# Token groups of 512, 512, 512, 384, 384 in place of 384, 512, 512, 512, 384, with the work order laid anew

## The chip, the cores and the metric

The kernel runs on one core of one Trainium2 chip. The metric is the device time of one execution in microseconds; the kernel before took 482.29 us (median of 3 runs, 481.82 to 482.75). The profile is of one more execution, which took 482.01 us; its span, from the first to the last instruction that the profile holds, is 480.2 us.

## The reference

Three layers follow one another, over 4 batches of 576 tokens (2304 in all) with 8 heads of 64, so 512 channels. `factor` is 4 and `scale` 1/8.

```
# 1. attention, twice: over tokens averaged by 4 (then repeated 4 times), and over neighbours |i-j| < 4
out_d = sm_attn(mean4(q), mean4(k), mean4(v));  out_up = repeat(out_d, 4)
scores = where(|i-j| < 4, scale * q @ k.T, -1e9);  attn = exp(scores - max) / (sum + 1e-9)
x = out_up + attn @ v                                   # (2304, 512)
# 2. gated layer: d_ff = 1536
x = ((x @ w_a) * (x @ w_b)) @ w_out                     # (2304, 512)
# 3. soft mixture of 8 experts with 4 slots each, F = 1024
logits = x @ phi                                        # (2304, 32)
d = softmax(logits, over tokens);  slot_in = d.T @ x    # (32, 512)
slot_out[e] = relu(slot_in[e] @ w1[e]) @ w2[e]
out = softmax(logits, over slots) @ slot_out            # (2304, 512)
```

w_a, w_b and w_out come as 64-bit numbers and are turned into 32-bit ones on the chip.

## The kernel before

**Attention** goes by pairs: each batch has five stretches of up to 116 tokens (`plan_pair`). A pair is scored on PE (L462, L472), reduced and exponentiated on DVE and ACT (L480 to L506), normalized on POOL or DVE (L293), transposed on PE (L516), multiplied with v on PE (L530), and added to the coarse attention of its batch (`xadd`, L541, DVE). Then x is split into a high part (a rounded copy, `xhi`) and the rest (a subtraction, `xlo`), on ACT, DVE or POOL. The coarse attention of a batch (`plan_datt`) must be done before its first pair is multiplied with v: its scores are L673, its exponentials L701 (ACT), its transposes L733 and L737, its product L784.

**The gated layer** goes by groups of tokens, `GS`, and 12 slices of 128 of d_ff. One unit (`plan_unit`) is a group and a slice: 12 matmuls for w_a and 12 for w_b (L1068), each 128 by the group's tokens, then a copy on ACT or DVE and a multiplication on DVE (L1083) into one of the chunks of the tile `gr`. A unit can begin when the whole group's x is there, so the first one waits for all pairs of the first group. The order in which a group takes its 12 slices is turned by `KO`, and `GO` says at which chunk of `gr` it begins.

**The weights** w_a and w_b come in 24 pieces of 512 KB (`plan_piece`): a DMA into a staging slot, two steps on ACT or DVE (`clow`, L877 or L879; `mag`, L883), one that joins them on DVE (L888), a rounded copy (`chi`, L288 or L290), and a subtraction (`clo`, L293, on POOL or DVE). Four pieces serve two units.

**The end**: after the last unit come the softmax over tokens, the slots' input (L1396), the experts (L1437, L1490) and the output (L1529). The experts' weights, 64 loads of 512 KB (L1343), go into buffers that the gated layer has left.

**The order** is written out: each step is a task with a number, `ORDER` lists all numbers, and each engine runs its tasks in that order; `OTHER` lists the tasks that run on their second engine. SP's queue of DMAs is in that order too. While PE has nothing to do in the first 60 us of the planner's count, the planner puts in matmuls on data that nobody reads (L347), as many as fill its own estimate of the gap; after the last unit it puts in others (L352).

Of the kernel before, what the change touches and what calls it, by code (L numbers as in the profile page):

```python
# [22 lines left out]
GS = [384, 512, 512, 512, 384]  # L23
# [4 lines left out]
GO = [0, 1, 0, 1, 0]  # L28
KO = [0, 6, 0, 9, 0]
NGC = 5  # L30
# [9 lines left out]
HEADS = [0, 2, 4, 6, 1, 3, 5, 7]  # L40
# [77 lines left out]
def rows_of(w):  # L118
    w = w.view(np.int64) if w.dtype == np.float64 else w
    return np.ascontiguousarray(w.reshape(8, 64, -1)[HEADS].reshape(w.shape))  # L120
# [128 lines left out]
def tile_attn_glu_softmoe(  # L249
# [16 lines left out]
    nc = tc.nc  # L266
    ctx.enter_context(tc.manual_schedule())
    P = Plan(dict(CAPS))
    add = P.add
# [38 lines left out]
    def c_dma(nbytes, wide=False):  # L308
        return nbytes / (400e3 if wide else 358e3)
# [15 lines left out]
    gr = mp.tile([128, NGC * 1536], F32, name="gr")  # L325
# [10 lines left out]
    T = {}  # L336
# [259 lines left out]
    def room_of(where):  # L596
        if where == "w8":
            return sb(wp, "w8", (128, 1024))
        if where == "sw":
            return X["sw"].pop(0).bitcast(F32)  # L600
        n = int(where[2:])
        return gr[:, n * 1536:n * 1536 + 1024]
# [264 lines left out]
    wsrc = (w_a, w_b)  # L867
# [25 lines left out]
    def plan_piece(n, key):  # L893

        fc, m = key[0], key[-1]
# [4 lines left out]
        def stage():  # L900
            X["raw", key] = s = X[where].pop(0)
            if isw:
                c0 = fc * 512 + key[2] * 256
                nc.sync.dma_start(
                    out=s.rearrange("p (m f) -> p m f", m=2),
                    in_=wsrc[key[1]][m * 256:m * 256 + 256, c0:c0 + 256].rearrange("(m p) f -> p m f", p=128),
                )
            else:
                nc.sync.dma_start(out=s, in_=w_outt[m * 128:m * 128 + 128, fc * 512:(fc + 1) * 512])
# [34 lines left out]
        o = CPR[n]  # L944
# [5 lines left out]
        if n == 0:  # L950
            T["stage"] = add("N", 0.0, rooms, (), -100, acq=("w8",) * CAPS["st"], lat=0.0)
        ts_ = add(
            "D", c_dma(524288), stage, [T["stage"]], prio=SOON[n] if n < len(SOON) else o - 1.5, acq=(where,), lat=2.0
# [99 lines left out]
    def plan_unit(g, k, n):  # L1053
        fc, fi = divmod(k, 4)
        gt = GS[g]
# [57 lines left out]
        tg = add("V", gt / 960 + 0.08, gmul, [tb, te, T.get(("gt", g, before))], -30, acq=tuple(f"gc{x}" for x in new), rel=("ps", "a", "un"))  # L1113
# [486 lines left out]
DE_AT = ["w8", "gc3", "sw", "sw"]  # L1600
PT_AT = ["w8", "gc4", "sw", "sw"]
# [11 lines left out]
def cpr(c):  # L1613
# [122 lines left out]
```

## Time and profile before

| | |
|---|---|
| median of 3 runs | 482.29 us |
| the profiled execution | 482.01 us |
| its span | 480.2 us |
| PE busy | 466.8 us, 97% |
| DVE, ACT, POOL busy | 269.4, 145.4, 121.6 us |
| first matmul of the gated layer, and the second | 38.05 us, 39.38 us |
| last matmul of the gated layer's last unit | issued at 420.4 us |
| moved by DMA | 84.26 MB |

The page gives the busy time of each engine, the chain of work that ended last, and groups of instructions by line. The tables by stretch of time give busy time, the clock granted to TensorE and the DMA engines' busy share. A matmul's end is modelled, so a time from the start of one instruction to the start of the next is more exact than a duration.

### The profile page before, as it was taken

Reading aid. Unit: us, or ns where it says so; the run is one execution under the profiler, and the core shown is the slowest. Engines: PE = TensorE matmul, PEld = TensorE weight load, DVE = VectorE, ACT = ScalarE, POOL = GpSimd, SP = SyncE. Lnnn points to the kernel's source line nnn. Section 1 sums busy time; section 2 is a strip of 40 time slices with the busy share of each in tenths; the row PEclk is TensorE's granted clock in tenths of the full one; section 3 lists DMA queues with packets and bytes.
Section 4 is the critical chain, followed back from the end, with each engine's and each line's share of the span. In section 5 each row is a group of like instructions: output and inputs, shape, how many; then the busy total and the mean of one; then the engine's idle time right before and its main releaser. Section 6 shows DMA issues by size and latency. Waiting matters only on the chain.

```text
span 480.2 us, 11383 instructions
## 1 busy us (share of the span) xinstructions
PE 466.8 (97%) x4755; PEld 363.0 (76%) x4755; DVE 269.4 (56%) x570; ACT 145.4 (30%) x392; POOL 121.6 (25%) x180
## 2 busy tenths in 40 slices
PE   7999999999999999999999999999999999999994
PEld 4778989887776777778788777788877879853462
DVE  3998997485658545678543249423525743460022
ACT  1878846514244311221320113002120210321132
POOL 4888985443055000454050011000000000010000
PEclk9999999999999999999999999999999999999998
DMA  8979843474651003223010010021236699899998
GB/s 303 389 264 306 291 132 115 139 240 176 217 173 45 2 1 114 58 65 128 12 46 0 18 50 1 3 87 45 97 129 240 216 363 377 283 346 410 407 407 322
DMA packets 30402, 84.26 MB, mean 175 GB/s; under 512 B 3472, under 2 KB 4240, under 8 KB 30352
## 3 DMA queue, kind: packets, MB, share of 16 engines
q1 hardware_dynamic: 30352, 83.54, 49.4%
q8 instruction: 37, 0.61, 0.5%
q14 instruction: 13, 0.11, 0.1%
HBM read 78.81 MB, written 4.72 MB: 174 GB/s over the span
## 4 chain that ended last, share of the span: by engine, by line
PE 84%; DVE 7%; ACT 4%; DMA 3%; issue 1%; SPq 0%; POOL 0%; ACTq 0%; DVEq 0%; POOLq 0%
PE ps L1068 58%; PE ps L1490 3%; PE ps L1437 3%; PE ps L1228 3%; PE ps L1093 3%; PE ps L530 2%; DMA w<-in_moe_w_dram 2%; PE ps L516 2%; DMA x<-in_qk_dram 1%; PE ps L784 1%; PE ps L673 1%; PE ps L472 1%; DVE dT L425 1%; PE ps L1529 1%; ACT ps L883 1%
## 5 line engine op out<-in xcount | busy, mean ns | idle before, releaser
L1068 PE MATMUL ps<-x,w 128*128 128x512 f32 (+1 forms) x1440 | 308.5, 371 | 1.2 <-DVE x L293 0.9
L1068 PEld LDWEIGHTS ps<-x,w 128*128 128x128 f32 x1440 | 259.8, 188 | 43.6 <-issue 5.5
L1083 DVE TENSOR_TENSOR gr<-a,ps 128x512 f32<-128x512 f32 (+1 forms) x60 | 37.7, 629 | 77.3 <-PE ps L1068 69.3
L288 ACT COPY a<-ps 128x512 f32<-128x512 f32 (+1 forms) x38 | 20.0, 534 | 95.8 <-PE ps L1068 93.9
L1101 DVE STREAM_TRANSPOSE gr<-gr 128x1024 f32<-128x1024 f32 (+2 forms) x31 | 33.1, 1089 | 5.3 <-PE ps L1093 5.3
L1215 POOL TENSOR_TENSOR cn<-lc,cs 128x128 f32<-128x128 f32 (+1 forms) x5 | 1.9, 380 | 133.1 <-DVE cs L1212 133.1
L293 POOL TENSOR_TENSOR x<-xn,x 128x464 fp32r<-128x464 f32 (+4 forms) x12 | 13.1, 1091 | 84.4 <-DVE x L290 73.6
L499 ACT ACTIVATE e<-e 128x512 f32<-128x512 f32 x20 | 12.6, 631 | 47.0 <-DVE e L492 47.0
L541 DVE TENSOR_TENSOR xn<-ps,xd 128x232 f32<-128x232 f32 (+1 forms) x40 | 13.8, 387 | 20.3 <-PE ps L530 19.9
L290 DVE COPY a<-ps 128x512 f32<-128x512 f32 (+1 forms) x22 | 14.1, 643 | 19.4 <-PE ps L1068 19.4
L293 POOL TENSOR_TENSOR w<-w,w 128x512 fp32r<-128x512 f32 x16 | 21.0, 1327 | 2.8 <-ACT w L288 2.5
L293 POOL TENSOR_TENSOR e<-e,mx 128x512 f32<-128x512 f32 x12 | 12.9, 1073 | 25.4 <-DVE mx L506 23.9
L347 PE MATMUL ps<-acc 128*128 128x512 f32 (+2 forms) x46 | 16.7, 494 | 2.2 <-POOL acc L340 2.2
L480 DVE TENSOR_REDUCE mx<-ps 128x4 f32<-128x256 f32 x40 | 14.7, 410 | 3.8 <-PE ps L472 3.8
L1228 PE MATMUL ps<-gr,lgs 32*32 32x384 f32 x576 | 16.3, 491 | 0.1
L530 PEld LDWEIGHTS ps<-e,bv 64*64 64x64 f32 x640 | 12.6, 133 | 4.9 <-issue 3.3
L425 DVE TENSOR_REDUCE dT<-qk 128x116 f32<-128x464 f32 (+1 forms) x20 | 12.0, 620 | 6.1 <-DMA qk<-in_qk_dram 6.1
L430 POOL TENSOR_TENSOR dT<-dT,qk 128x116 f32<-128x116 f32 (+1 forms) x28 | 14.7, 524 | 2.2
L530 PE MATMUL ps<-e,bv 64*64 64x58 f32 (+1 forms) x640 | 14.9, 226 | 0.1
L347 PEld LDWEIGHTS ps<-acc 128*128 128x128 f32 x46 | 8.7, 207 | 8.1 <-issue 5.2
L883 ACT ACTIVATE ps<-sw 128x512 f32<-128x512 f32 x18 | 11.4, 633 | 11.0 <-DVE xn L541 4.8
L492 DVE TENSOR_TENSOR e<-ps,mx 128x256 f32<-128x256 f32 x40 | 14.7, 409 | 0.0
(204 smaller groups left out, 568.9 us busy)
## 6 DMA issues: line engine op xcount, KB each, us to landing
w<-in_moe_w_dram SPq DMA_DIRECT2D x32, 512.0 KB, 8.7
qk<-in_qk_dram SPq DMA_DIRECT2D x17, 480.0 KB, 4.7
sw<-in_w_outt_dram SPq DMA_DIRECT2D x12, 512.0 KB, 3.8
w8x<-in_moe_w_out_dram SPq DMA_DIRECT2D x12, 512.0 KB, 3.7
x<-in_moe_w_dram SPq DMA_DIRECT2D x11, 512.0 KB, 7.9
w<-in_moe_w_a_dram SPq DMA_DIRECT2D x10, 512.0 KB, 7.3
bv<-in_vw_dram SPq DMA_DIRECT2D x20, 256.0 KB, 3.3
w8x<-in_moe_w_dram SPq DMA_DIRECT2D x10, 512.0 KB, 9.9
```

The lines of the kernel that those rows point to most:

```text
L288: nc.scalar.copy(out=out, in_=in_)
L293: (nc.vector if e == "V" else nc.gpsimd).tensor_tensor(**a)
L347: nc.tensor.matmul(out=X["warm"][:, 0:128 * w], lhsT=x[:, 0:128], rhs=x[:, 0:128 * w], start=True, stop=True)
L425: nc.vector.tensor_reduce(out=dst, in_=view(src, dims, off), op=ALU.add, axis=AX.X)
L430: nc.gpsimd.tensor_tensor(out=dst, in0=dst, in1=one[r], op=ALU.add)
L480: nc.vector.tensor_reduce(out=mx[:, hl], in_=X["s", n, hl], op=ALU.max, axis=AX.X)
L530: nc.tensor.matmul(out=pss[hl][o:o + 64, hq // 2, bi * w:bi * w + w], lhsT=v[r, bi, hq, :], rhs=pt[r, hq, 1 + bi * 64:1 + bi * 64 + w], st ...
L883: nc.scalar.activation(out=f, in_=words(raw)[0].bitcast(F32), func=ACTF.Prelu, scale=2.0 ** -112, alpha=-(2.0 ** 32))
L1068: nc.tensor.matmul(out=ps, lhsT=X["w", fc, ab, fi // 2, wi][:, fi % 2, hq, :], rhs=X[x, g][:, hq, :], start=(hq == 0 and m == 0), stop=(hq ...
L1083: nc.vector.tensor_tensor(out=X["g", g][:, k, :], in0=X.pop(("a", g, k)), in1=X.pop(("mm", g, k, 1)), op=ALU.mult)
L1101: nc.vector.transpose(out=t, in_=t)
L1228: nc.tensor.matmul(out=ps[q][o:o + 32, :], lhsT=d[r, b, :], rhs=g[r, :, b * 32:b * 32 + 32], start=(b < 4), stop=(b >= gt // 32 - 4),)
```

## The change

The first group has 512 tokens in place of 384 and the fourth 384 in place of 512. `GO`, `KO` and the order of the tasks are set anew, and some tasks go to other engines. A piece of w_a or w_b is now laid out on the host so that it is one run of 4 KB for each of the 128 partitions; before it was two runs of 2 KB. Since the first group now takes four chunks of `gr`, only the fifth is left beside it for buffers of the first pairs' batches: two of these are both put into the fifth chunk, at its start (up to 704) and behind (704 to 1280), with a new token `gp4` that the second group's unit takes when it begins to use that chunk.

```diff
-GS = [384, 512, 512, 512, 384]
+GS = [512, 512, 512, 384, 384]
-GO = [0, 1, 0, 1, 0]
-KO = [0, 6, 0, 9, 0]
+GO = [0, 1, 0, 2, 0]
+KO = [0, 9, 0, 8, 0]
 def rows_of(w):
     w = w.view(np.int64) if w.dtype == np.float64 else w
-    return np.ascontiguousarray(w.reshape(8, 64, -1)[HEADS].reshape(w.shape))
+    w = w.reshape(8, 64, -1)[HEADS].reshape(2, 2, 128, 3, 2, 256)
+    return np.ascontiguousarray(w.transpose(3, 4, 0, 2, 1, 5)).reshape(-1, 512)
 def room_of(where):
-        n = int(where[2:])
-        return gr[:, n * 1536:n * 1536 + 1024]
+        n = int(where[2:]) * 1536
+        return gr[:, n + 704:n + 1280] if where[1] == "p" else gr[:, n:n + 704]
 def stage():
-                c0 = fc * 512 + key[2] * 256
-                nc.sync.dma_start(
-                    out=s.rearrange("p (m f) -> p m f", m=2),
-                    in_=wsrc[key[1]][m * 256:m * 256 + 256, c0:c0 + 256].rearrange("(m p) f -> p m f", p=128),
-                )
+                r0 = (fc * 4 + key[2] * 2 + m) * 128
+                nc.sync.dma_start(out=s, in_=wsrc[key[1]][r0:r0 + 128, :])
 def plan_unit(g, k, n):
-  acq=tuple(f"gc{x}" for x in new)
+  acq=tuple(f"gc{x}" for x in new) + (("gp4",) if g == 1 and int(PT_AT[1][2:]) in new else ())
-DE_AT = ["w8", "gc3", "sw", "sw"]
-PT_AT = ["w8", "gc4", "sw", "sw"]
+DE_AT = ["w8", "gc4", "sw", "sw"]
+PT_AT = ["w8", "gp4", "sw", "sw"]
 ORDER = [
-    5, 8, 7, 11, 0, 1, 2, 10, 6, 12, 9, 14, 15, 3, 59, 61, 17, 13, 529, 16, 18, 530, 74, 76, 20, 62, 19, 27, 29, 37,
+    11, 5, 8, 7, 6, 12, 1, 0, 9, 529, 15, 10, 13, 18, 14, 3, 2, 59, 530, 27, 17, 61, 20, 16, 532, 531, 19, 21, 29, 62,
...
-CAPS.update({f"gc{x}": 1 for x in range(NGC)})
+CAPS.update({f"gc{x}": 1 for x in range(NGC)}, gp4=1)
```

The orders below leave times out. In the changed kernel the line numbers up to 904 are one higher, and those of the gated layer two lower (L1068 is L1066, L1529 is L1527).

PE before, the last rows ahead of the first unit (the band's four short matmuls that stand before each score of 16 are left out): v products (`e,bv`), scores (`qk`), transposes (`cst,e`) and matmuls on unread data (`acc`).

```order
L347 MATMUL ps<-acc 128x512
L347 MATMUL ps<-acc 128x256
L347 MATMUL ps<-acc 128x128
L530 MATMUL ps<-e,bv 64x58 x16
L516 MATMUL ps<-cst,e 128x128 x4
...
L472 MATMUL ps<-qk 58x64 x16
L530 MATMUL ps<-e,bv 64x58 x16
...
L472 MATMUL ps<-qk 58x64 x16
L347 MATMUL ps<-acc 128x256
L347 MATMUL ps<-acc 128x128
L1068 MATMUL ps<-x,w_277 128x384 x2
```

The same place in the changed kernel.

```order
L348 MATMUL ps<-acc 128x256
L348 MATMUL ps<-acc 128x128
L517 MATMUL ps<-cst,e 128x128 x4
...
L473 MATMUL ps<-qk 58x64 x16
L348 MATMUL ps<-acc 128x128
L531 MATMUL ps<-e,bv 64x56 x16
L348 MATMUL ps<-acc 128x256
L348 MATMUL ps<-acc 128x128
...
L473 MATMUL ps<-qk 58x64 x16
L1066 MATMUL ps<-x,w_345 128x512 x2
```

Ahead of the first unit there now stand a fifth v product (the one of 56 columns), a fifth transpose of a pair and an eighth score (before: four, four and seven). Counted in 128 columns, the `acc` matmuls ahead of it are 63 (before 57), of them 22 behind the first v product (before 13).

DVE before, around the first unit: the last x subtraction of the first group is `x<-xn,x 128x4x36`; `w` rows belong to the weights' pieces.

```order
L888 SCALAR_TENSOR_TENSOR w_143<-ps,w_143 128x512
L541 TENSOR_TENSOR xn<-ps,xd 128x232 x2
L888 SCALAR_TENSOR_TENSOR w_148<-ps,w_148 128x512
L290 CAST x<-xn 128x4x36
L293 TENSOR_TENSOR x<-xn,x 128x4x36
L425 TENSOR_REDUCE dT_684<-qk 128x4x29
L480 TENSOR_REDUCE mx<-ps 128x4 x2
L888 SCALAR_TENSOR_TENSOR w_144<-ps,w_144 128x512
L888 SCALAR_TENSOR_TENSOR w_145<-ps,w_145 128x512
```

DVE in the changed kernel, from the last x subtraction of the first group on.

```order
L294 TENSOR_TENSOR w_618<-w_103,w_617 128x2x256
L542 TENSOR_TENSOR xn<-ps,xd 128x2x112 x2
L291 CAST x<-xn 128x4x48
L294 TENSOR_TENSOR x<-xn,x 128x4x48
L426 TENSOR_REDUCE dT_435<-qk 128x4x29
L889 SCALAR_TENSOR_TENSOR w_105<-ps,w_105 128x512
L294 TENSOR_TENSOR w_746<-w_102,w_745 128x2x256
L889 SCALAR_TENSOR_TENSOR w_101<-ps,w_101 128x512
L291 COPY a<-ps 128x512
L889 SCALAR_TENSOR_TENSOR w_100<-ps,w_100 128x512
L294 TENSOR_TENSOR w_810<-w_105,w_809 128x2x256
L294 TENSOR_TENSOR w_746<-w_101,w_745 128x2x256
```

Up to the last x subtraction DVE has joined five weight pieces (before seven). In the whole program 11 of the weights' subtractions (`w` from `w` or `sw`) run on DVE (before 3); POOL has 13 (before 21).

PE at the end of the program, the changed kernel first: expert matmuls (`acc`), output matmuls (`cn,ht`), and the sum over experts of the last 128 columns (`a,cst`).

```order
L1527 MATMUL ps<-cn,ht 128x288 x4
L1488 MATMUL ps<-w_4645,acc 32x128 x8
L1488 MATMUL ps<-w_4078,acc 32x128 x8
L1488 MATMUL ps<-w_4079,acc 32x128 x8
L1488 MATMUL ps<-w_4230,acc 32x128 x8
L1527 MATMUL ps<-cn,ht 128x288 x4
L1508 MATMUL ps<-a,cst 128x128
L1527 MATMUL ps<-cn,ht 128x288 x8
```

Before, the rows from the second expert piece on were these.

```order
L1529 MATMUL ps<-cn,ht 128x288 x4
L1490 MATMUL ps<-w_4267,acc 32x128 x8
L1490 MATMUL ps<-x,acc 32x128 x8
L1490 MATMUL ps<-w_4599,acc 32x128 x8
L1490 MATMUL ps<-w_4526,acc 32x128 x8
L1510 MATMUL ps<-a,cst 128x128
L1529 MATMUL ps<-cn,ht 128x288 x8
```

Four output matmuls moved from before the expert matmuls to behind them, ahead of the sum over experts.

## Rows read from the trace of the kernel before

**Rows 1.** The page, part 1: busy us, share of the span, instructions.

```profile
PE 466.8 (97%) x4755; PEld 363.0 (76%) x4755; DVE 269.4 (56%) x570; ACT 145.4 (30%) x392; POOL 121.6 (25%) x180
```

**Rows 2.** Stretches: length; PE, PEld, DVE, ACT, POOL busy; clock; DMA share; GB/s.

```profile
10.00:20.00 10.00, 10.00 (x127) 7.21 (x118) 9.66 (x28) 6.62 (x28) 8.09 (x18) 1.00 1.05 391
...
30.00:39.40 9.40, 7.88 (x196) 6.14 (x193) 8.88 (x21) 7.39 (x15) 7.66 (x9) 1.00 0.96 322
...
50.00:60.00 10.00, 10.00 (x120) 9.68 (x119) 9.80 (x21) 8.73 (x17) 9.60 (x12) 1.00 0.87 273
```

**Rows 3.** Waits of PE between 39 and 110 us: us, times, longest.

```profile
PE ps L1068 <- DVE x L293: 0.9, 1, 0.9
PE ps L673 <- DVE dT L425: 0.6, 1, 0.6
PE ps L733 <- DVE gr L293: 0.3, 1, 0.3
```

**Rows 4.** PE in order of time up to 40 us: start, us, idle before.

```profile
27.91 0.72 PE L530 MATMUL ps<-e,bv 64*64 64x58 f32 x30
...
29.68 0.66 PE L516 MATMUL ps<-cst,e 128*128 128x128 f32 x4
30.17 0.82 PE L347 MATMUL ps<-acc 128*128 128x256 f32 x4
30.92 0.31 PE L462 MATMUL ps<-band,eyeb 64*64 64x256 bf16 x4
...
31.60 1.78 PE L347 MATMUL ps<-acc 128*128 128x512 f32 x6
33.31 0.75 PE L530 MATMUL ps<-e,bv 64*64 64x58 f32 x32
...
38.05 0.41 PE L1068 MATMUL ps<-x,w 128*128 128x384 f32 x1
39.38 10.47 PE L1068 MATMUL ps<-x,w 128*128 128x384 f32 x59 [0.92 <-DVE x L293]
```

**Rows 5.** ACT between 13 and 24 us, in order of time.

```profile
14.88 0.19 ACT L698 ACTIVATE dn<-dn 128x2 f32<-128x2 f32 x1
...
16.08 0.68 ACT L877 ACTIVATE w<-w 128x512 uint32<-128x512 uint32 x1
```

**Rows 6.** The chain that ended last: start, us; pieces of the gated layer's matmuls.

```profile
71.65 6.47 PE ps L1068 x36
...
91.42 2.31 PE ps L1068 x12
...
119.93 2.95 PE ps L1068 x12
...
172.78 11.11 PE ps L1068 x48
```

**Rows 7.** Groups by line and shape: busy us, mean ns; idle before.

```profile
L293 DVE TENSOR_TENSOR w<-w,w 128x512 fp32r<-128x512 f32 x2 | 2.6, 1324 | 0.0
```

**Rows 8.** DVE in order of time, up to 112 us.

```profile
37.93 1.30 DVE L293 TENSOR_TENSOR x<-xn,x 128x144 fp32r<-128x144 f32 x1
...
50.51 1.24 DVE L888 SCALAR_TENSOR_TENSOR sw<-ps,sw 128x512 uint32<-128x512 uint32 x2
...
63.55 1.13 DVE L425 TENSOR_REDUCE dT<-qk 128x112 f32<-128x448 f32 x2
...
72.74 0.69 DVE L293 TENSOR_TENSOR w<-sw,w 128x512 fp32r<-128x512 f32 x1
```

**Rows 9.** Stretches late in the program, columns as in rows 2.

```profile
410.00:421.00 11.00, 11.00 (x65) 9.88 (x63) 4.63 (x10) 3.73 (x13) 0.00 (x0) 1.00 0.81 271
...
440.00:450.00 10.00, 10.00 (x108) 3.59 (x104) 0.23 (x1) 1.79 (x3) 0.00 (x0) 1.00 1.02 407
```

**Rows 10.** PE in order of time, from 275 us on.

```profile
282.38 1.07 PE L1093 MATMUL ps<-gr,wpr 128*32 128x512 f32 x8
...
472.18 0.49 PE L1510 MATMUL ps<-a,cst 128*128 128x128 f32 x2 [0.55 <-ACT a L1506]
```

More of the change, by code (lines that the diff above doesn't have):

```diff
@@ L952, in plan_piece @@
         ts_ = add(
-            "D", c_dma(524288), stage, [T["stage"]], prio=SOON[n] if n < len(SOON) else o - 1.5, acq=(where,), lat=2.0
+            "D", c_dma(524288, True), stage, [T["stage"]], prio=SOON[n] if n < len(SOON) else o - 1.5, acq=(where,), lat=2.0
         )
@@ L1112, in plan_unit @@
         T.setdefault(("mmw", fc, 1, fi // 2), []).append(tb)
-        tg = add("V", gt / 960 + 0.08, gmul, [tb, te, T.get(("gt", g, before))], -30, acq=tuple(f"gc{x}" for x in new), rel=("ps", "a", "un"))
+        tg = add("V", gt / 960 + 0.08, gmul, [tb, te, T.get(("gt", g, before))], -30, acq=tuple(f"gc{x}" for x in new) + (("gp4",) if g == 1 and int(PT_AT[1][2:]) in new else ()), rel=("ps", "a", "un"))
         T["gt", g, k] = tg
```

137 rows, old and new, of tables (ORDER, OTHER) are left out of this document.

## The prediction

> **What bounds the kernel now.** I read the page's first part, then the table of stretches, the waits of PE, and PE in order of time. PE is busy for 97% of the span [rows 1]; between 39 and 110 us it waits three times, 1.8 us in all [rows 3], and the first of these, 0.92 us, stands right at the first unit of the gated layer [rows 4]. So from the first unit on the time is the sum of PE's work, and that sum the change leaves as it is: three groups of 512 and two of 384 in any sequence make 864 matmuls of 512 columns and 576 of 384. A run of the gated layer's matmuls that another step breaks costs more than its matmuls: from 12 to 48 of 512 columns the time goes from 2.95 to 11.11 us, 0.227 each, so 12 alone cost 0.23 over that; for 384 it is 0.173 each and again 0.23 [rows 6]. Fewer breaks would count, but counted in the order there are 40 such runs before and 40 after, so this term is zero. What is left is time that PE spends on nothing: ahead of the first unit, in waits of the first group, and at the end.
>
> **The start.** Until 39 us DVE is the fullest engine (9.66 of 10 us, then 8.88 of 9.4), with POOL and ACT not far behind [rows 2]; PE fills up with matmuls on unread data. The first unit's matmuls run from 39.38 us on, with one done before, which makes 39.2 us [rows 4]. The changed kernel needs a fifth pair before it can begin, and its order puts in front a v product, a transpose and a score more. These cost 0.75 us (the v product at 33.31), 0.49 (29.68 to 30.17) and 0.68 (30.92 to 31.60) [rows 4], together 1.92. They are not lost: they would come later anyway. What counts is how much later than 39.2 + 1.9 = 41.1 us the first unit begins.
>
> First v product: 27.91 us before [rows 4]; it waits for the first batch's coarse attention, whose exponentials on ACT begin with the step at 14.88 us and are broken once by a weight step of 0.68 us [rows 5]. In the new order the three sets of exponentials follow one another, and the averages ahead of them have fewer steps on DVE in front (one reduction of a score less, a pair's reduction less); that I put at 0.68 + 0.6, so 26.6 us. The 0.6 is a choice between 0 and the 0.9 that such steps last; with 0 it is 27.2.
>
> From there the new order has on PE five v products, five scores, three transposes and 22 blocks of 128 unread columns. A block is 0.244 us (seven of them from 31.60 to 33.31) [rows 4]. Sum: 5 x 0.75 + 5 x 0.68 + 3 x 0.49 + 22 x 0.244 = 14.0 us, so 40.6 us if nothing waits. The same sum for before (4, 4, 2 and 13) gives 9.9 from 27.91, 37.8 us, against the 39.2 measured: 1.4 us of waits on DVE and POOL. I let the new start have 0.2 of these, because DVE has less in front of it (five weight pieces joined in place of seven, 0.6 us each, against the fifth pair's sum, cast and subtraction). First unit: 40.8 us, 0.3 before the 41.1. Bounds: 40.6, a gain of 0.5, and 27.2 + 14.0 + 1.4 = 42.6, a loss of 1.5. Term: -0.3.
>
> **Whole slots.** A piece brings the same 512 KB. No wait of PE in the first group ends at a DMA [rows 3], so a quicker landing is hidden behind DVE, which is full. Beside it, at the rates of two stretches, 391 and 407 GB/s [rows 2, 9], a piece takes 1.34 or 1.29 us: 12 pieces ahead of the first unit would land 0.6 us sooner at most. Taken: 0; ends 0 and -0.6. SP's queue has the same pieces in it, and the first qk loads of batch 1 stand behind fewer of them.
>
> **The first group.** Its units now take 24 x 0.227 = 5.4 us in place of 24 x 0.173 = 4.2, so two units give the weights' engines 10.9 us for four pieces where they gave 8.3. On the other side two pieces fewer are joined when it begins, and eight subtractions more are DVE's. The tightest place in the new order is the second batch's first coarse scores, which stand on PE behind 60 matmuls and wait for the last average of that batch on DVE. PE is there 60 x 0.227 + 0.2 = 13.8 us after the first matmul. DVE has in that time 6 joins at 0.62 and 5 averages at 0.57 (two took 1.24, two 1.13) [rows 8], and 4 subtractions, 2 multiplications, a copy and three smaller steps, which I put at 0.6 each but for one at 0.33: 3.7 + 2.9 + 4.2 + 1.5 = 12.3 us. That leaves 1.5 us if nothing holds a subtraction up. In this trace something does: two of DVE's three weights' subtractions took 1.32 us [rows 7], one 0.69, and one of only 144 columns took 1.30 while POOL was at a subtraction of its own [rows 8]. At two in three, 4 x 0.63 x 2/3 = 1.7 us, PE waits 0.2; with all four, 2.5 and 1.0. The next place, the second slices' w_b, has 120 matmuls in front (28.9 us with the steps between) and is not late by this count. Before, this stage had two waits, 0.6 for such an average and 0.3 [rows 3]. Term: 0.3 - 0.9 = -0.6; ends -0.9 and +0.3.
>
> The Trainium skill, "SBUF — State Buffer", section "Who interferes with whom", says that a VectorE tensor_tensor with both inputs in SBUF contends with GpSimd's reads, and that whichever of the two comes second waits for the whole other instruction. The trace agrees (1.30 us for 144 columns). By the rule each of these subtractions that meets POOL at work is held up, which is the slower rival below.
>
> **The middle.** Behind the last v product of a group's x, the order has two scores and other steps before the next group's first matmul. At the fourth group it is closest: its second pair's v product stands 3.5 us (two scores at 0.68 [rows 4] and two blocks of logits at 1.07 [rows 10]) ahead of its first unit, and DVE has between them the pair's sum, a multiplication, a transposition and the subtraction, 2.9 us by the same spacing. I put 0.2 there, ends 0 and 1.3. The new token on the fifth chunk is free in time: the product that gives it back stands 84 matmuls ahead of the second group.
>
> **The end.** With a shorter fourth group the last pairs' x comes nearer to the end, and with it the first buffers for the experts; but in both orders 31 of the 64 expert loads stand in SP's queue ahead of the last unit's end, and in the stretch before it the DMA engines were 81% busy [rows 9], so they can make up for it. At the very end PE waits 0.55 us for ACT before the sum over experts of the last columns [rows 10]; four output matmuls now stand in that gap. Term: -0.5, ends 0 and -0.7.
>
> **Sum.** -0.3 + 0 - 0.6 + 0.2 - 0.5 = -1.2 us against the profiled execution's own 482.01, so 480.8. The median of the runs is 0.28 above that execution: 481.1 us.
>
> **Rivals.**
> - Ports (slower). DVE and POOL hold each other up until the first unit: the last rows of both ahead of it are subtractions with two inputs in SBUF, POOL's four of x, DVE's of a weight and of x. Then the new start is at its upper bound, 42.6 us in place of 40.8, and the coarse scores wait 1.0 in place of 0.2: 481.1 + 1.8 + 0.8 = 483.7. For it: three of the four such rows that I have [rows 7, 8]. Against: before, DVE was 94% busy in the last stretch [rows 2] and yet began within 1.4 us of the plain sum. It decides from a first unit at about 42.3 us on.
> - All slack (faster). The first unit at its earliest, with pieces that land sooner (-0.5 - 0.3), no wait in the first group (-0.9), none in the middle, 0.7 at the end: 482.29 - 2.4 = 479.9. For it: 10.9 us where 8.3 nearly sufficed. Against: DVE was full until 60 us [rows 2].
> - The fourth group waits for its x, 1.3 us in place of 0.2, because DVE's transposition stands in front of the subtraction: 482.2, the same as before. For it: 0.6 us of room. Against: no group start before shows a wait of this kind but the first.
> - The pieces as whole slots bring nothing because the rate stays: the forecast stands, since I count them at nothing.
>
> **How the numbers follow.** Forecast 0.41, ports 0.20, all slack 0.24, fourth group 0.15. What this kernel's measurement can tell from no change is about 0.2%, 0.96 us: faster is below 481.33, slower above 483.25. The forecast's own range is 480.4 to 481.9; of its 0.41, 0.24 is faster and 0.17 the same. Ports: 0.16 slower, 0.04 the same. All slack is faster. Fourth group: 0.12 the same, 0.03 slower. Faster 0.48, same 0.33, slower 0.19. The range takes in the ports and nearly all of the slack: 479.4 to 484.2.
>
> **What would show it.** In the profile after: the first 512-column matmuls at 40.8 us (40.6 to 42.6); DVE's weights' subtractions at a mean between 0.9 and 1.2 us; one wait of PE for the average (L425), 0.2 us, and at most one of 0.5 at a group's start; the gated layer's matmuls at the same 0.227 and 0.173 each; from the last unit's end to the end of the span 0.5 us less than before. I am wrong if the stretch from the second group's first matmul to the last unit, at equal work, differs by over 1 us, or if the first unit begins later than 42.6.

## The result and the profile after

The changed kernel took 485.20 us (median of 5 runs, 484.21 to 486.38), beside 482.29 for the kernel before in as many runs: 1.0065 times its time, 95% interval 1.0042 to 1.0088. I had forecast 481.1 and a range up to 484.2. It is slower, and outside the range.

The two profiled executions differ by 3.19 us (485.20 and 482.01), and the traces place all of it. The last gated unit's matmuls end where the next step begins: 420.56 us before, 422.18 after.

| stretch, us | before | after | difference |
|---|---|---|---|
| to the second matmul of the gated layer before, the first after | 39.38 | 42.02 | +2.64 |
| from there to the end of the last gated unit | 381.18 | 380.16 | -1.02 |
| from there to the end of the span | 59.64 | 61.12 | +1.48 |
| around the span | 1.81 | 1.90 | +0.09 |

About 1.9 us of TensorE's work moved from the second stretch to the first, so the three are some 0.7, 0.9 and 1.5 us worse than the plain shift. First, PE's products with v, one block on unread data (L348) and the first gated unit of the kernel after, in order of time (start, us, idle before):

```profile
27.11 0.75 PE L531 MATMUL ps<-e,bv 64*64 64x58 f32 x32
...
32.84 0.74 PE L531 MATMUL ps<-e,bv 64*64 64x58 f32 x32
...
36.01 0.75 PE L531 MATMUL ps<-e,bv 64*64 64x58 f32 x32
...
38.66 0.49 PE L348 MATMUL ps<-acc 128*128 128x128 f32 x2
39.08 0.74 PE L531 MATMUL ps<-e,bv 64*64 64x56 f32 x32
...
42.02 2.32 PE L1066 MATMUL ps<-x,w 128*128 128x512 f32 x8 [0.25 <-ACT ps L884]
```

From the first product to the first unit it is 14.91 us here and 11.47 before [rows 4]. A pair more takes one step of the sequence, 3.07 to 3.17 us (32.84 to 36.01 to 39.08): 1.9 us of its own matmuls, and matmuls on unread data that fill PE while the pair's chain runs through VectorE, ScalarE and GpSimd. PE itself waits only 0.25 us in these 14.91. That the chain needs the whole step is not shown: ScalarE's copy of the transposed pair ended at 35.96 for the product at 36.01, but at 38.73 for the one at 39.08, with a block on unread data still ahead of it (38.66), and no run left such blocks out.

All waits of PE in the kernel after, over the whole span (us, times, longest; before, three of them in the first group are rows 3):

```profile
PE ps L348 <- POOL acc L341: 2.2, 1, 2.2
PE ps L734 <- POOL gr L294: 1.5, 1, 1.5
PE ps L517 <- DVE e L294: 0.4, 1, 0.4
PE ps L1527 <- ACT ht L1513: 0.4, 1, 0.4
PE ps L463 <- DVE w L889: 0.3, 1, 0.3
PE ps L1066 <- ACT ps L884: 0.2, 1, 0.2
```

The wait for an average that I had looked for is not there. In its place the transposes of the second batch's coarse attention (L734, at 81.39) wait 1.45 us for their normalization. Where that comes from is seen on VectorE and GpSimd, in order of time:

```profile
69.82 4.11 DVE L294 TENSOR_TENSOR w<-w,w 128x512 fp32r<-128x512 f32 x4
...
76.49 0.77 DVE L687 TENSOR_REDUCE dn<-ps 128x2 f32<-128x288 f32 x2
```

```profile
69.13 3.05 POOL L294 TENSOR_TENSOR w<-w,w 128x512 fp32r<-128x512 f32 x2
...
79.68 1.66 POOL L294 TENSOR_TENSOR gr<-gr,dm 128x128 f32<-128x128 f32 x2 [0.79 <-DVE dm L710]
```

The scores were on PE at 70.79 us; their maximum (L687) stood behind four weights' subtractions. The two that met GpSimd's took 1.20 and 1.79 us and the two behind them 0.68 each, as one before (0.69 [rows 8]); GpSimd's two took 1.34 and 1.77. A copy, a fifth subtraction, a join and a sum, 2.6 us, stood behind those.

Then the end. Stretches from 410 us on, of the kernel before and then of the kernel after (length, clock, the DMA engines' busy share, GB/s):

```profile
410.00:420.56 10.56, 1.00 0.79 268
420.56:430.00 9.44, 1.00 0.97 332
430.00:460.00 30.00, 1.00 1.03 409
460.00:474.00 14.00, 1.00 1.02 403
474.00:476.00 2.00, 1.00 0.74 292
476.00:478.00 2.00, 0.83 1.00 391
478.00:480.20 2.20, 0.50 0.23 87
```

```profile
410.00:422.18 12.18, 1.00 1.02 380
422.18:430.00 7.82, 1.00 1.00 336
430.00:460.00 30.00, 1.00 1.03 406
460.00:474.00 14.00, 1.00 1.02 403
474.00:476.00 2.00, 1.00 0.94 371
476.00:478.00 2.00, 0.96 1.03 403
478.00:480.00 2.00, 0.50 0.95 372
480.00:483.30 3.30, 0.50 0.12 46
```

From the last unit on, the transfers never pause in the kernel after, and hardly before. PE's last matmul ends at 474.27 before and 475.01 after, 0.74 apart; the ends of the spans are 3.1 apart. Rate by length gives what is moved from the last unit on: 22.6 MB before (3.13 + 12.27 + 5.64 + 0.58 + 0.78 + 0.19), 22.9 after. In both, 33 of the 64 expert loads are issued after that unit, since they wait for slots of 4 KB a partition that the gated layer gives back.

### The profile page after: what moved, and what is told of

The parts are those of the page before. It is cut to its first block, busy times and chain, and to the rows that moved or that the text cites. A ratio compares the mean times of both kernels' runs of the same rounds, so it can differ in the third digit from the quotient of the medians.

```text
span 483.3 us, 11365 instructions
## 1 busy us (share of the span) xinstructions
PE 469.8 (97%) x4763; PEld 364.7 (75%) x4763; DVE 273.1 (57%) x569; ACT 147.8 (31%) x396; POOL 115.2 (24%) x180
## 2 busy tenths in 40 slices
DMA packets 27330, 84.26 MB, mean 174 GB/s; under 512 B 3472, under 2 KB 4240, under 8 KB 27280
## 4 chain that ended last, share of the span: by engine, by line
PE 88%; DVE 5%; POOL 2%; ACT 2%; issue 1%; DVEq 0%; POOLq 0%; ACTq 0%
PE ps L1066 57%; PE ps L1226 3%; PE ps L348 3%; PE ps L1488 3%; PE ps L1435 3%; PE ps L1091 3%; PE ps L531 3%; PE ps L517 2%; PE ps L785 2%; PE ps L473 2%; PE ps L674 1%; PE ps L1527 1%; DVE w L294 1%; PE ps L937 1%; PE ps L353 1%
## 5 line engine op out<-in xcount | busy, mean ns | idle before, releaser
L1066 PE MATMUL ps<-x,w 128*128 128x512 f32 (+1 forms) x1440 | 308.5, 371 | 0.3 <-ACT ps L884 0.2
L1066 PEld LDWEIGHTS ps<-x,w 128*128 128x128 f32 x1440 | 259.5, 188 | 43.6 <-issue 7.9
L294 POOL TENSOR_TENSOR x<-xn,x 128x464 fp32r<-128x464 f32 (+4 forms) x15 | 16.1, 1074 | 85.0 <-DVE x L291 63.4
L291 DVE COPY a<-ps 128x512 f32<-128x512 f32 (+1 forms) x28 | 17.3, 621 | 21.3 <-PE ps L1066 21.2
L289 ACT COPY a<-ps 128x512 f32<-128x512 f32 (+1 forms) x32 | 17.5, 549 | 36.4 <-PE ps L1066 36.3
L348 PE MATMUL ps<-acc 128*128 128x128 f32 (+2 forms) x54 | 19.3, 483 | 2.2 <-POOL acc L341 2.2
L884 ACT ACTIVATE ps<-w8x 128x512 f32<-128x512 f32 x12 | 7.6, 631 | 34.9 <-DMA w8x<-in_moe_w_out_dram 29.6
L431 POOL TENSOR_TENSOR dT<-dT,qk 128x116 f32<-128x116 f32 (+1 forms) x34 | 17.0, 499 | 2.7
L348 PEld LDWEIGHTS ps<-acc 128*128 128x128 f32 x54 | 10.0, 206 | 9.0 <-issue 5.9
L289 ACT CAST x<-xn 128x464 fp32r<-128x464 f32 (+6 forms) x16 | 8.1, 511 | 28.3 <-DVE xn L542 28.3
L687 DVE TENSOR_REDUCE dn<-ps 128x2 f32<-128x288 f32 (+1 forms) x24 | 8.5, 397 | 12.1 <-PE ps L674 12.0
```

The source lines that it names most:

```text
L289: nc.scalar.copy(out=out, in_=in_)
L291: (nc.vector if e == "V" else nc.gpsimd).tensor_copy(out=out, in_=in_)
L294: (nc.vector if e == "V" else nc.gpsimd).tensor_tensor(**a)
L348: nc.tensor.matmul(out=X["warm"][:, 0:128 * w], lhsT=x[:, 0:128], rhs=x[:, 0:128 * w], start=True, stop=True)
L431: nc.gpsimd.tensor_tensor(out=dst, in0=dst, in1=one[r], op=ALU.add)
L884: nc.scalar.activation(out=f, in_=words(raw)[0].bitcast(F32), func=ACTF.Prelu, scale=2.0 ** -112, alpha=-(2.0 ** 32))
```

## Experiments

Theory A: the end is the last gated unit plus the transfers that still wait there, at about 400 GB/s; PE, its order and the evictions behind it do not count. Theory B, its rival, is what my prediction had assumed: PE's work and the steps behind it set the end. Ratios are to the kernel before, with 95% intervals; the "stretches" are read from each run's trace as in the table above.

**Fewer bytes out, in both kernels.**

```diff
-                            m = (n - n0 + 1) * 288
+                            m = 288
```

> The changed kernel, with each of the 12 output transfers cut to its first third or half (288 of 864 or 576 columns; two thirds of the output are not written). Theory A (transfers): from the last gated unit (422.2 us) on the DMA engines are never free (share 1.00 to 1.03, 400 to 408 GB/s, until 480), so the end is set by the bytes that are left then, and 2.4 MB less (5.8 us at 408 GB/s) shortens it until the matmuls and evictions set it: last eviction 476.2, issue 477.4, a transfer in the clear about 2.2, end about 479.6 instead of 483.3: 3 to 4 us less, about 481.8. Theory B (engines): the end hangs on the last matmuls and evictions, and fewer bytes give at most 0.5 us: about 484.8.

> The same cut of the output transfers in the kernel before. Theory A: there the DMA share falls to 0.74 between 474 and 476 us, so the transfers are only just behind; the end goes from 480.2 to about 478.5 (last eviction 475.7, issue 476.3, 2.2 for a transfer in the clear): 1.2 to 1.8 us less, about 480.8. The gap between the two kernels then shrinks from 2.9 to about 1. Theory B: at most 0.5 us less, and the gap stays at 2.9.

The edit keeps 288 columns of each of the twelve output transfers; 81.31 MB are moved in place of 84.26, so it takes out 2.95 MB (the expectation's 2.4 should read so).

Measured: 479.81 us for the changed kernel (0.9960, 0.9946 to 0.9973), 478.59 for the one before (0.9934, 0.9920 to 0.9947). That is 5.4 and 3.4 us less than uncut; the gap between the kernels falls from 2.9 to 1.2. B is out. The kernel before gained twice what I expected: it too was bound by transfers. Late stretches of the changed kernel so cut (columns as above):

```profile
460.00:474.00 14.00, 1.00 0.85 321
474.00:476.00 2.00, 1.00 0.65 209
476.00:478.00 2.00, 0.77 0.24 77
```

The share falls under 1 long before the span's end at 478.2. From the last unit to the end it is now 56.07 us for the changed kernel and 57.46 before: with the transfers out of the way, the new order of the end is 1.4 us shorter.

**Less work for PE at the end, in both kernels.**

```diff
                     for e in range(4):
+                        if dh == 2 and 0 < eg * 8 + f < 15:
+                            X.pop((1, dh, eg, f, e))
+                            continue
                         nc.tensor.matmul(
```

> The changed kernel without 56 of the 64 last matmuls of the expert output (columns 384 to 511 of the output are wrong); at 1.0 us for 32 that is 1.7 us of TensorE right before the last output. All transfers stay. Theory A: the last output transfers are ready 1.7 us earlier but stand behind others, so the end moves by 0 to 0.5 us (484.7 to 485.2). Theory B: 1.5 to 1.7 us less (about 483.6).

> The same 56 matmuls left out of the kernel before. Theory A: only the gap in its transfers between 474 and 476 us (0.26 of 2 us) can be filled: 0.3 to 0.8 us less (about 481.7). Theory B: 1.5 to 1.7 us less (about 480.7).

Measured: 485.10 (1.0075, 1.0056 to 1.0093) and 481.87 (0.9996, 0.9985 to 1.0007): neither moves. The trace of the first shows where PE's saving went, a wait for the weights of the matmuls that stayed:

```profile
471.02 0.43 PE L1491 MATMUL ps<-w,acc 128*32 128x128 f32 x8 [1.90 <-DMA w<-in_moe_w_dram]
```

**The end's order set back**: in the changed kernel the tasks from the first late load on stand in the order of the kernel before (`ORDER`, and `OTHER` for the evictions), but for one transposition of the logits.

> The changed kernel, with the order of the expert stage (its loads, matmuls, evictions and which engine evicts) as in the kernel before. Theory A (transfers): the same bytes are left at the last gated unit, so the end stays within 0.7 us of 485.2, though the last matmul comes about 0.5 us later. Rival D (the new order of loads, evictions and outputs costs the 1.5 us that the stretch from the last gated unit to the end grew by): about 483.7.

Measured: 485.14 (1.0062, 1.0044 to 1.0079); last unit to end 61.55 us. Rival D is out: the end's new order neither costs nor gives anything that can be measured.

**A slot more, a slot less.** The loads' pool `w8x` gets 11 or 9 slots in place of 10; for the 11th, one of two buffers `ht` and one of three in each of the small pools `cs` and `cm` go, two small tiles move to another pool, and two activations move behind the transposes that free the other `ht`.

```diff
-    cs=3, w8x=10, e4=0,
+    cs=2, w8x=11, e4=0,
-    eyeb = cp.tile([128, 64], BF16, name="eyeb")
+    eyeb = at.tile([128, 64], BF16, name="eyeb")
...
```

> The kernel before, with one slot of 4 KB a partition more for the expert loads (11 instead of 10 in their pool; the room comes from one of two buffers for the expert stage's hidden rows, and from two small tiles that are moved to a pool which is given back). Every load takes a slot that came free one release earlier. Theory A (bytes left): 32 loads instead of 33 wait for the last gated unit, 0.5 MB less is left there (22.1 instead of 22.6 MB), the 2.2 us that the transfers idle between 410 and 420.6 take it up, and the end comes 0.6 to 1.3 us earlier: about 480.9. Rival E (engines and order): no change, or up to 0.3 more for the two activations that wait for the one buffer.

> The kernel before with one slot less for the expert loads (9). Theory A: 0.5 MB more is left at the last gated unit, and the end comes 0.8 to 1.3 us later: about 482.9. Rival E: no change.

> The same slot added to the changed kernel. Theory A: 0.5 MB less is left at the last gated unit, but the transfers idle only 0.05 to 0.12 of the time from 390 to 410 there and not at all from 410 on, so 0.3 to 1.0 us earlier: about 484.4. Rival E: no change.

Measured, for the kernel before: a slot more 481.47 (0.9982, 0.9965 to 0.9999), a slot less 483.40 (1.0022, 1.0005 to 1.0038), the signs and nearly the sizes of theory A (-0.9 and +1.1 us by the ratios). Stretches of the two, first the one with 11:

```profile
420.03:430.00 9.97, 1.00 0.98 339
430.00:479.50 49.50, 0.98 0.96 379
```

```profile
419.56:430.00 10.44, 1.00 0.98 350
430.00:480.70 50.70, 0.94 0.97 385
```

They hold 22.1 MB and 23.2 MB, 0.5 to either side of 22.6, and last 59.47 and 61.14 us, to either side of the 59.64 to 60.42 of three executions without this edit. The slot less has its last unit 1 us earlier than the profiled execution of before and its end 0.5 later. So what is left at the last unit sets the end. For the changed kernel a slot more gave 484.37 (1.0051, 1.0032 to 1.0070): the sign is A's, but the interval overlaps the 1.0065 of no edit, and in its profiled execution the end was no shorter (61.32), so this one decides nothing.

**The start, one subtraction on another engine.** In the changed kernel the cast of the first group's last 192 columns on VectorE took 1.21 us while GpSimd was at a subtraction:

```profile
40.66 1.21 DVE L291 CAST x<-xn 128x192 fp32r<-128x192 f32 x1
```

```profile
40.44 1.31 POOL L294 TENSOR_TENSOR w<-w,w 128x512 fp32r<-128x512 f32 x1
```

Task 556, that subtraction, is added to `OTHER`.

> The changed kernel, with the one weight subtraction that GpSimd runs from 40.44 to 41.75 us put on VectorE, behind the cast and the subtraction of the first group's last 192 columns. Theory P (the two engines hold each other up): the cast took 1.21 us beside it, where 128x144 took 0.30 in the kernel before; it ends 0.7 to 0.8 earlier and the first unit begins at 41.2 to 41.5 instead of 42.02; the end 0.5 to 0.8 earlier: about 484.5. Theory Q (ScalarE's two activations into PSUM that end at 42.00 release the first unit): first unit at 42.0, and the end within 0.3 of 485.2.

Measured: 485.10 (1.0059, 1.0039 to 1.0079), no gain. The mechanism shows: the cast now reads

```profile
41.38 0.29 DVE L291 CAST x<-xn 128x192 fp32r<-128x192 f32 x1
```

and from the first product with v to the first unit it is 14.41 us in place of 14.91, without any wait of PE: what is left there is PE's own steps, the matmuls on unread data among them. But in this execution the wait at the transposes is 2.31 us, and the granted clock falls behind it (length, PE busy, clock):

```profile
81.00:82.00 1.00, 0.00 (x0) 1.00 0.79 305
82.00:83.00 1.00, 0.42 (x4) 1.00 0.56 217
83.00:84.00 1.00, 1.00 (x8) 0.67 0.07 27
84.00:85.00 1.00, 1.00 (x9) 0.50 0.00 0
```

**The one wait in the first group.** First the maximum and the exponentials earlier (tasks 170 to 172 of `ORDER`, and 173 ahead of 227), then the normalization (173) also ahead of a weight subtraction (669); the second is shown:

```diff
-861, 662, 667, 226, 170, 859, 668, 671, 171, 156, 864, 172, 673, 159, 669, 863, 672, 674, 227, 173
+861, 170, 171, 662, 667, 226, 859, 172, 668, 671, 156, 864, 673, 159, 173, 669, 863, 672, 674, 227
```

> The changed kernel, with the maximum of the first chunk of the second batch's coarse scores taken ahead of a weight subtraction, a bit join and a sum on VectorE instead of behind them, its exponentials ahead of a cast on ScalarE, and its normalization ahead of that of a fine chunk on GpSimd. Theory A (the end is the last gated unit plus the transfers that are left then): the one wait of 1.45 us in the first group (81.39 us) goes, the last gated unit comes 1.2 to 1.5 us earlier, and the end as much: about 483.8. Rival C (slack taken elsewhere): what was moved behind is late next (a gated unit waits for its weights, or the fine chunk's product for its normalization) and gives back half or more: 484.5 to 485.2.

> As the run with the maximum taken earlier, and the coarse normalization of the second batch's first chunk now also ahead of the weight subtraction that GpSimd ran before it (78.32 to 79.65 us there, with the normalization's input ready at 78.24). Theory A (the end follows the last gated unit): the normalization ends at about 79.9, the wait that was 1.45 in the changed kernel and 1.03 in that run falls under 0.3, the stretch from first unit to last gated unit goes from 380.2 to 378.7 to 379.0, and the end 1.0 to 1.4 earlier than the changed kernel's: about 484.0. Rival C: the subtraction that now comes later holds a gated unit, and the stretch stays at 380.

Measured: 484.37 (1.0053, 1.0034 to 1.0071), then 484.89 (1.0062, 1.0043 to 1.0082). The first leaves 1.03 us of the wait, since GpSimd takes a subtraction (78.32 to 79.65) before the normalization. The second takes that wait away, and its trace has these in its place:

```profile
PE ps L1066 <- ACT gr L289: 0.6, 1, 0.6
...
PE ps L1066 <- DVE sw L889: 0.4, 1, 0.4
```

From first to last unit it is 380.07 and 380.12 us, against 380.16. The traces fit rival C: in this group the three engines are full, and a place given to one step is taken from another. The runs do not settle it: their intervals overlap the 1.0065 of no edit, and the stretch varies by over 1 us where none of its tasks was moved. With the end's order set back it was 379.44 us and the wait 0.78, in the changed kernel without whole slots (below) 379.67 and 0.66; with the slot more it was 380.63 and 1.47.

**Both in the changed kernel**, with the last columns' low half on GpSimd ahead of that weight subtraction (task 132):

> As the run before in this list, and the last 192 columns of the first group's low half subtracted on GpSimd, ahead of the weight subtraction that held up VectorE's cast there (1.21 us for 128x192). Theory P with A: from the first product with v to the first unit 14.9 us becomes 14.3 to 14.5, and the end another 0.4 to 0.6 earlier: about 483.5. Rival: the weight subtraction, 0.5 us later, holds the first unit's second half, or its saving is waited away in the first group: 484.0 as in the run before. Either way it stays over the 481.8 of the kernel before, since the extra chunk ahead of the first unit (1.1 us over its 1.95 of TensorE) and the longer end (1.2 us) remain.

Measured: 484.54 (1.0043, 1.0025 to 1.0061). First product to first unit 14.16 us, again without a wait of PE and with one block on unread data fewer; first to last unit 379.92, with waits of 0.7 and 0.4 us in place of the 1.45.

**The same move in the kernel before** (task 116 to GpSimd, ahead of its two weight subtractions):

> The kernel before, with the last 144 columns of the first group's low half subtracted on GpSimd, ahead of the two weight subtractions beside which VectorE took 1.30 us for it. Theory P with A: the first unit's wait of 0.9 us goes to 0.1 or 0.2, from the first product with v to the first unit 11.47 us becomes 10.7, and the end comes 0.5 to 0.8 earlier: about 481.2, faster than both kernels. Rival C: the weight subtractions end 0.6 later, and a unit behind the first waits as much: 481.8, no change.

Measured: 481.17 (0.9984, 0.9975 to 0.9994): faster than both kernels. The first unit no longer waits (rows 4 and 8 show the 0.92 us and the 1.30 us of before):

```profile
37.66 0.50 POOL L295 TENSOR_TENSOR x<-xn,x 128x144 fp32r<-128x144 f32 x1 [0.20 <-DMA w<-in_moe_w_b_dram]
37.74 0.19 PEld L1070 LDWEIGHTS ps<-x,w 128*128 128x128 f32 x1
37.77 3.49 PE L1070 MATMUL ps<-x,w 128*128 128x384 f32 x17
```

First product to the run of the first unit: 10.09 us in place of 11.47, where one of its matmuls (0.17) was already done, so 1.2 us less. How much of it the first group takes back can't be told: from there to the last unit it is 381.41, and with that matmul added 380.7 to 381.5 in six executions without the edit.

**Whole slots alone, and the changed kernel without them.**

> The kernel before with the weights' pieces as whole slots alone (their layout in device memory and their transfers; order and everything else as before). If TensorE's start hangs on the pieces' arrival, up to 0.6 us less (481.4); if not, within 0.3 of before. The end's transfers are others, and don't change.

> The changed kernel with the weights' pieces in the old layout, two runs of 1 KB a row instead of whole slots (everything else as changed). From the same edit alone in the kernel before, which changed nothing (ratio 1.0002, 0.9988 to 1.0016): within 0.3 us of 485.2. If the pieces' arrival sets the start here, 0.3 to 0.8 us more.

Measured: 481.77 (1.0002, 0.9988 to 1.0016) and 484.03 (1.0049, 1.0031 to 1.0066; overlapping the 1.0065 with them). This edit is worth nothing here that can be measured. (The expectation's 1 KB should read 2 KB.)

**The two gains joined**, in the kernel before: the slot and the move to GpSimd.

> The kernel before with both: the slot more, and the last 144 columns of the first group's low half on GpSimd (which gave ratio 0.9984). If the two add up, 1.2 to 1.9 us faster than before: about 480.2. If the loads take up the time that the earlier last unit gives, only the larger of the two: about 480.9.

Measured: 480.44 us (0.9970, 0.9955 to 0.9986), some 1.4 us faster than before and 4.6 faster than the changed kernel by the ratios. They add up, nearly.

## Why the prediction was wrong

**What bounds the kernel** is the step that failed. I wrote that from the first unit on the time is the sum of PE's work. That holds up to the last gated unit. Behind it PE is as busy as ever, but in time with the transfers: a busy engine is not yet the one that sets the end. The row stood there, 407 GB/s at a share of 1.02 for 440 to 450 us [rows 9], and I read only the stretch before it, with its 0.81, as room to catch up.

**The end** (term -0.5, measured +1.48) fell with it. On PE the term was more than right: from the last unit to PE's last matmul it is 53.71 us before and 52.83 after. The runs with the outputs cut show the gain, 1.4 us; with whole outputs it is hidden, and the run with the old order shows no difference. What lengthened the end is 0.3 MB more that was left at the last unit (0.7 us at 408 GB/s); the rest, about 0.8, lies in rates a little lower at its two edges, and no run isolates it. The sign repeats, the size is that of one pair of executions: without an edit of the end this stretch lasts 59.64 to 60.42 us in three executions of before and its variants (22.6 to 22.7 MB), and 60.56 to 62.22 in six of the changed kernel and its variants (22.8 to 22.9).

**The start** (term -0.3, measured +0.9 against the 41.1 I had set, 0.7 against 39.38 + 1.92). The waits were about what I had put, 0.3 us for 0.2: from the first product to the first unit PE is busy for 14.59 of 14.91 us, before for 9.95 of 11.47. Two other parts were off. The earlier first product (27.11; I put 26.6) lies within what varies from one execution to the next: in the executions of the experiments it lies between 27.10 and 27.98 for variants of the kernel before and between 26.48 and 27.93 for those of the changed one, while the interval from it to the first unit repeats within 0.04 us wherever the start is not edited. And the sum of PE's own steps was too small, 14.0 us for the 14.59 that PE is busy: I had priced all 22 blocks on unread data at the 0.244 of seven in one run, and a block that stands alone takes 0.42 (38.66 to 39.08). The 22 take 6.3 us for my 5.4, the other steps 0.3 less than put. By the repeated interval the start is 3.43 us later, 1.5 more than PE's moved work; whether the chains of five pairs need that time, or the blocks put in to fill it take it, stays open.

**The first group and the middle** (terms -0.6 and +0.2, together measured +0.7). The place that I called tightest had no wait. The wait came one step on, 1.45 us, where the maximum of the same scores stood behind four subtractions, two of which met GpSimd's. So PE's waits in the first group went from 0.9 us [rows 3] to 1.45, where I had put 0.3. I had weighed this mechanism, at two in three and as the slower rival; it is a part of what that rival said, at another place. The two runs that took the wait away by the order got others for it; in the two executions where it came out shorter without a move in this group (0.78 and 0.66 us) the stretch was 0.5 to 0.7 us shorter too. So the wait costs about its length, as far as single executions show, and these edits only moved it. The fourth group began without a wait, and nothing stops PE from 110 us to the last unit but for 0.09 us.

**Runs that are broken, whole slots** (0 and 0): right; the latter by two runs.

**What I had named as a sign** would not have caught it. The first unit at 42.02 was within 42.6, and VectorE's eleven weights' subtractions had a mean of 0.84 us, under the 0.9 to 1.2 that I had named. The line on the end, half a us less, was plainly wrong, but I had listed it as a sum of PE's, not as the place where the rest would vanish.

**The sizes**: +2.64, -1.02, +1.48 and +0.09 make the 3.19 of the two executions, worked out after the fact. Shown by runs are the transfers at the end (by four edits) and the two engines' mutual hold at the start (by two). That the first group has no slack fits two runs and is not shown. The 3.1 us of a pair are read from the trace alone, and what sets them is open.

## What to carry to other kernels

Ask of each stretch which resource has no pause there, and whether the busy engine leads it or follows it; where transfers run at their full rate to the end, count the bytes that are left when the last buffer comes free, and work for another free buffer before work for a shorter order. Where several engines feed the first step, add up the leading engine's whole interval, its fillers included, each at the price of the form in which it stands; an item more can cost the pace of its whole chain, which here stayed open. A wait that is taken away among full engines can come back at the next step.

## What the runs showed of the hardware

- VectorE's cast, with one input in SBUF, was held up by GpSimd's subtraction: 1.21 us beside it, 0.29 in the run where that subtraction was on VectorE; it ended at 41.87, just behind GpSimd's 41.75. The Trainium skill, "SBUF — State Buffer", section "Who interferes with whom", lists casts among the instructions that can take the pair of ports that the two engines share, and says that the second to come waits for the whole of the first. The trace agrees, by these times.
- Subtractions with two inputs in SBUF, on both engines at once, took turns: GpSimd's ran from 69.13 to 70.47 and from 70.41 to 72.18 us, VectorE's from 69.82 to 71.02 and from 70.94 to 72.73. Each of VectorE's ended 0.55 us behind the one of GpSimd that it met; alone it takes 0.68.
- A wait of PE of 2.31 us was followed by a granted clock of 0.50 (1.2 GHz in place of 2.4) from about 83.3 to 86.7 us. Waits of 1.45 to 1.50 us at the same place in four other executions left it at 1.00. That this is why single executions of the changed kernel lie some 2 us apart was not shown.
- One core's transfers held 397 to 409 GB/s from 430 to 460 us, in every trace here, beside full matmul work.
